# An FNet and GEGLU stack whose scheduler orders by the deadlines of a dry run, with raw operands loaded six items ahead

## The chip, the cores and the metric

The kernel runs on one core of a Trainium2 chip. The metric is the device time of one execution in microseconds; a verdict compares medians of several executions. Times inside an execution come from one profiled execution, whose own time is given beside its span below.

## What is computed

Two kinds of layer alternate, four in all, on `x` of 2048 x 512 in fp32:

```python
def _A_ref(x, dft_seq_re, dft_seq_im, dft_hid_re, dft_hid_im):
    a = jnp.einsum("bsd,ed->bse", x, dft_hid_re)
    b = jnp.einsum("bsd,ed->bse", x, dft_hid_im)
    return jnp.einsum("ts,bse->bte", dft_seq_re, a) - jnp.einsum("ts,bse->bte", dft_seq_im, b)
def _B_ref(x, w_gate, w_up, w_down):
    return (_gelu(x @ w_gate) * (x @ w_up)) @ w_down
x = A_x
x = x + _A_ref(_layernorm(x), ...)    # layer 0
x = x + _B_ref(_layernorm(x), ...)    # layer 1
x = x + _A_ref(_layernorm(x), ...)    # layer 2
x = x + _B_ref(_layernorm(x), ...)    # layer 3
```

The sequence matrices are 2048 x 2048, the hidden ones 512 x 512, gate and up 512 x 1792, down 1792 x 512.

## The kernel before

**Arithmetic.** TensorE works on fp32 operands that are split in two: ScalarE writes the rounded high part (line 140), VectorE subtracts it from the source for the low part (line 141), and `mm3` (lines 174 to 176) adds high x high, high x low and low x high in a PSUM bank. A matmul here takes a 128x128 stationary part and a 128x512 moving part. There are 7034 matmuls in the program, 7002 of them from `mm3`; this text numbers them from 0 in the order in which TensorE runs them.

**Mix layers (0 and 2).** The product with the sequence matrices is done by blocks of seven products in place of eight (Strassen's scheme in Winograd's form). For each of four column blocks b there are the stages A11 and A12, then S2 (with S1 and S3), S4, and between them the products with the hidden matrices (`hid_groups`). All operand blocks of 128x512 fp32 (256 KB) come from memory: `ws` and `wh`. Sums and differences of `ws` blocks are made on VectorE (lines 162 and 165) before they are split. While block b = 3 runs S2 and S4, the normed rows of the next layer come back from memory transposed, as 32 transfers of 64 KB per half (`fetch`, line 612, tensor `t`), and are combined and split too.

**GEGLU layers (1 and 3).** Gate and up are done by seven products per pair of blocks; two halves w of 1024 rows each. The down product is done by seven products for most of the hidden blocks, and by plain products for the rest (`plain_rows`): its first rows wait for `begun` partial sums, which `rows_done` (line 1155, issued by POOL) writes out and `begun_load` (line 1169) reads back in another layout. Eight rows of PSUM results are then added to x (`x_add`, line 165 with a PSUM operand). At the end of layer 1 these rows are normed for layer 2 (lines 494 to 499 and 516, with POOL taking the power at lines 497 and 498) and combined.

**Buffers.** SBUF holds 94 slots of 128x512 (`Slots`, a first-in first-out free list run while the program is traced), and two wide tiles that are lent as eight more (`wide`, `xwide`). PSUM has 8 banks. A tile may be written when the last reader of what was in its slot is done, so a load waits for a matmul or for VectorE.

**The order of the work.** Operands are a list of items in order of use. `split_next` loads up to `RAW` items beyond the one that it splits (`load_next` issues them on SP, line 272), and `take` lets splits run `AHEAD` = 7 items ahead of use. That is the order of the trace. A scheduler then reorders it: it runs the program on a model of the machine and each engine takes the ready instruction that stands first. `machine_as_traced` sets constants of that model: the gap between matmuls and the delay from the issue of a transfer on SP to its start. What comes out is one fixed order for each engine and queue; on the chip every engine runs its own in order and waits on semaphores. So an instruction that waits holds up all behind it on its engine.

Of the kernel before, what the change touches and what calls it, by code (L numbers as in the profile page):

```python
# [24 lines left out]
GELU_C = 0.044715  # L25
AHEAD = 7
MORE = 8
RAW = 4
WARM = 16
LAG = 6  # L30
NEAR = 3, 2, 6
# [7 lines left out]
LEAD = 3  # L39
NK = NS // 2  # L40
PASS_GAP_NS = 13.34
SP_DELAY_NS = 1900


@with_exitstack
def fnet_geglu(ctx: ExitStack, tc: tile.TileContext, x_in, ws, wh, wgu, wdn, wdc, out):
# [216 lines left out]
    def load_next():  # L263
        n = stream["loaded"]
        dtype, addresses, _, _ = items[n]
        raws[n] = []
        for a in addresses:
            t = sb.get(dtype)
            to = t if dtype == F32 else f32(t)
            if len(a.shape) == 3:  # L270
                to = to.rearrange("p (h c) -> p h c", h=2)
            stream["last"] = nc.sync.dma_start(to, a)
            raws[n].append(t)
        stream["loaded"] += 1

    def too_far(n):

        return items[n][2] is whole and n > stream["used"] + items[n][3]

    def split_next():  # L280
        n = stream["split"]
        while stream["loaded"] <= min(n + RAW, len(items) - 1) and not too_far(stream["loaded"]):
            load_next()
# [1047 lines left out]
@contextmanager  # L1331
def machine_as_traced():

    from concourse import hw_specs

    spec = hw_specs.TRN2Spec
    kept = {name: getattr(spec, name) for name in ("PE_FULL_CLOCK_PASS_GAP_NS", "DGE_DMA_DELAY")}
    spec.PE_FULL_CLOCK_PASS_GAP_NS = PASS_GAP_NS
    spec.DGE_DMA_DELAY = {**spec.DGE_DMA_DELAY, mybir.EngineType.SP: SP_DELAY_NS}
    try:  # L1340
        yield
    finally:
        for name, value in kept.items():
            setattr(spec, name, value)
# [43 lines left out]
```

## Time and profile before

| what | value |
|---|---|
| median of three executions | 1645.92 us (1640.87 to 1645.96) |
| profiled execution, its own time | 1644.12 us |
| its span, first to last instruction | 1642.2 us |
| TensorE busy | 1618.0 us, 99% of the span |
| VectorE busy | 1169.2 us, 71% |
| ScalarE busy | 827.5 us, 50% |
| GpSimd (POOL) busy | 229.2 us, 14% |
| moved by DMA | 424.15 MB, mean 258 GB/s |
| mean granted TensorE clock | 0.993 |

TensorE's matmuls overlap: each is shown with its full duration, and the next one starts before it ends. So the number of matmuls in a stretch of time, against the number in a stretch that has no gap, says more than the busy share. "Idle before" of a row is the time that the engine stood still ahead of it, and the arrow names what ended the wait.

### The profile page before, as it was taken

What the parts mean: (1) busy time and instruction counts of PE and PEld (TensorE: products, weight loads), DVE (VectorE), ACT (ScalarE), POOL (GpSimd) and SP (SyncE); (2) the same over time, 40 slices, a digit from 0 to 9 for tenths busy, and PEclk for the clock granted to TensorE, in tenths of its full rate; (3) what the DMA queues carried; (4) which work ended last, traced back from release to release, by engine and by line L of the source; (5) the groups of instructions that cost most, each with busy time, mean ns of one, the idle gap of its engine ahead of it and who ended that gap; (6) DMA issues with size and microseconds to landing.
All of it is one profiled execution on the core that took longest, in us unless ns stands there. A gap on an engine that the chain in (4) does not pass through costs nothing.

```text
span 1642.2 us, 22851 instructions
## 1 busy us (share of the span) xinstructions
PE 1618.0 (99%) x7066; PEld 1329.3 (81%) x7066; DVE 1169.2 (71%) x2009; ACT 827.5 (50%) x1605; POOL 229.2 (14%) x421
## 2 busy tenths in 40 slices
PE   9999999999999999999989999999899999999998
PEld 6888888878788888888878888888688888788887
DVE  8998878778776665657787977787754556944573
ACT  7754454544765535547585533544344545533360
POOL 3111010203544122220230000000001000010002
PEclk9999999999999999999999999999999999999999
DMA  9778787889877799977858777777789676896455
GB/s 363 254 242 275 237 274 230 283 280 359 316 271 263 234 372 368 334 249 237 248 187 299 229 229 241 265 243 259 235 283 312 211 221 184 275 293 204 147 174 154
DMA packets 252106, 424.15 MB, mean 258 GB/s; under 512 B 28816, under 2 KB 91024, under 8 KB 250960
## 3 DMA queue, kind: packets, MB, share of 16 engines
q1 hardware_dynamic: 227232, 336.95, 64.7%
q0 software_dynamic: 24752, 85.74, 14.2%
q8 instruction: 56, 0.92, 0.2%
q14 instruction: 66, 0.54, 0.1%
HBM read 336.86 MB, written 85.72 MB: 257 GB/s over the span
## 4 chain that ended last, share of the span: by engine, by line
PE 79%; DVE 7%; DMA 6%; issue 2%; POOL 1%; ACT 1%; SPq 0%; DVEq 0%; POOLq 0%; ACTq 0%
PE p L174 26%; PE p L175 26%; PE p L176 26%; DVE s L141 4%; DMA s<-ws 1%; DVE s L162 1%; DVE s L165 1%; DMA s<-t 1%; DMA s<-x 1%; DMA out<-s 1%; DMA xwide<-ws 1%; DMA s<-wgu 1%; DMA s<-begun 0%; DMA begun<-wide 0%; DMA begun<-xwide 0%
## 5 line engine op out<-in xcount | busy, mean ns | idle before, releaser
L175 PE MATMUL p<-s,s 128*128 128x512 f32 x2334 | 909.8, 391 | 1.4 <-DVE s L141 1.4
L174 PE MATMUL p<-s,s 128*128 128x512 f32 x2334 | 893.6, 391 | 15.2 <-DVE s L165 7.9
L176 PE MATMUL p<-s,s 128*128 128x512 f32 x2334 | 900.4, 390 | 0.0
L140 ACT ACTIVATE s<-s 128x512 fp32r<-128x512 f32 (+1 forms) x762 | 436.7, 607 | 459.0 <-DVE s L162 143.9
L141 DVE TENSOR_TENSOR s<-s,s 128x512 fp32r<-128x512 f32 (+1 forms) x762 | 482.6, 661 | 103.8 <-ACT s L140 70.3
L174 PEld LDWEIGHTS p<-s,s 128*128 128x128 f32 x2334 | 439.8, 188 | 113.0 <-DVE s L165 10.1
L175 PEld LDWEIGHTS p<-s,s 128*128 128x128 f32 x2334 | 439.8, 188 | 93.9 <-DVE s L141 2.5
L176 PEld LDWEIGHTS p<-s,s 128*128 128x128 f32 x2334 | 439.9, 188 | 91.9 <-issue 0.2
L165 DVE TENSOR_TENSOR s<-s,p 128x512 f32<-128x512 f32 x287 | 192.4, 681 | 174.8 <-PE p L176 79.4
L162 DVE TENSOR_TENSOR s<-s,s 128x512 f32<-128x512 f32 (+1 forms) x310 | 187.2, 618 | 39.7 <-DMA s<-ws 29.9
L169 ACT ACTIVATE s<-p 128x512 f32<-128x512 f32 x214 | 124.8, 590 | 105.6 <-PE p L176 102.7
L903 ACT ACTIVATE s<-s 128x512 f32<-128x512 f32 x103 | 64.8, 629 | 84.1 <-DVE s L165 77.7
L140 ACT ACTIVATE s<-xwide 128x512 fp32r<-128x512 f32 (+1 forms) x96 | 58.6, 617 | 46.8 <-PE p L175 15.6
L141 DVE TENSOR_TENSOR s<-xwide,s 128x512 fp32r<-128x512 f32 (+1 forms) x96 | 64.4, 676 | 14.4 <-ACT s L140 12.2
L497 POOL TENSOR_SCALAR rstd<-rstd 128x1 f32<-128x1 f32 x48 | 17.5, 365 | 392.9 <-ACT s L496 383.8
L165 DVE TENSOR_TENSOR s<-s,s 128x512 f32<-128x512 f32 (+1 forms) x70 | 42.9, 614 | 36.3 <-DMA s<-wgu 19.9
L256 POOL DMA_DIRECT2D wb<-s x84 | 45.8, 547 | 57.2 <-ACT s L140 27.5
L917 DVE TENSOR_TENSOR s<-s,s 128x512 f32<-128x512 f32 x75 | 51.7, 690 | 1.9
L516 ACT ACTIVATE s<-s,shift,rstd 128x512 f32<-128x512 f32 x55 | 44.2, 809 | 7.6 <-DVE shift L489 5.9
L218 POOL DMA_DIRECT2D x<-s x39 | 21.3, 548 | 170.8 <-DVE s L165 169.3
L494 ACT ACTIVATE s<-s 128x512 f32<-128x512 f32 x39 | 24.4, 626 | 36.5 <-DMA s<-x 23.4
L598 DVE STREAM_TRANSPOSE wide<-s 128x512 f32<-128x512 f32 x30 | 21.2, 706 | 25.2 <-ACT s L516 21.2
(98 smaller groups left out, 527.4 us busy)
## 6 DMA issues: line engine op xcount, KB each, us to landing
s<-ws SPq DMA_DIRECT2D x379, 256.0 KB, 4.4
s<-wb SPq DMA_DIRECT2D x294, 256.0 KB, 4.7
s<-wc SPq DMA_DIRECT2D x119, 256.0 KB, 4.3
s<-wh SPq DMA_DIRECT2D x116, 256.0 KB, 4.6
wb<-s POOLq DMA_DIRECT2D x98, 256.0 KB, 4.8
s<-x SPq DMA_DIRECT2D x63, 256.0 KB, 4.8
xwide<-ws SPq DMA_DIRECT2D x58, 256.0 KB, 4.1
wc<-s POOLq DMA_DIRECT2D x49, 256.0 KB, 5.7
```

The lines of the kernel that those rows point to most:

```text
L140: nc.scalar.activation(hi, src, AF.Copy)
L141: nc.vector.tensor_tensor(lo, src, f32(hi), op=ALU.subtract)
L162: nc.vector.tensor_tensor(out, a, b, op=ALU.subtract)
L165: nc.vector.tensor_tensor(out, a, b, op=ALU.add)
L169: nc.scalar.activation(v, src, AF.Copy)
L174: nc.tensor.matmul(ps, ah, bh, start=start, stop=False, skip_group_check=True)
L175: nc.tensor.matmul(ps, ah, bl, start=False, stop=False, skip_group_check=True)
L176: nc.tensor.matmul(ps, al, bh, start=False, stop=stop, skip_group_check=True)
L256: nc.gpsimd.dma_start(a, f32(t))
L516: nc.scalar.activation(z, x, AF.Identity, bias=shift, scale=rstd)
L903: nc.scalar.activation(t, g, AF.Gelu_apprx_tanh)
L917: nc.vector.tensor_tensor(t, t, v, op=ALU.mult)
```

## The change

Four things change. `RAW` goes from 4 to 6. The modelled delay of a transfer on SP goes from 1900 to 3000 ns. The modelled issue queue of VectorE and ScalarE becomes one instruction deep (12 before, by the model's default). And the context is made with `auto_bufs=True`: the scheduler first makes a dry run in the order of the trace, works out from it by when each instruction must have been issued at the latest, and in the final run each engine takes, among its ready instructions, the one with the earliest such deadline; it also assigns the tiles' addresses anew. Nothing else differs, and lines below 42 move down by one, those in and below `machine_as_traced` by more.

```diff
-RAW = 4
+RAW = 6
...
-SP_DELAY_NS = 1900
+SP_DELAY_NS = 3000
+DEPTH = 1
...
-    kept = {name: getattr(spec, name) for name in ("PE_FULL_CLOCK_PASS_GAP_NS", "DGE_DMA_DELAY")}
+    kept = {name: getattr(spec, name) for name in ("PE_FULL_CLOCK_PASS_GAP_NS", "DGE_DMA_DELAY", "ENG_ISSUE_QUEUE_DEPTH")}
     spec.PE_FULL_CLOCK_PASS_GAP_NS = PASS_GAP_NS
     spec.DGE_DMA_DELAY = {**spec.DGE_DMA_DELAY, mybir.EngineType.SP: SP_DELAY_NS}
+    depth = {mybir.EngineType.DVE: DEPTH, mybir.EngineType.Activation: DEPTH}
+    spec.ENG_ISSUE_QUEUE_DEPTH = {**spec.ENG_ISSUE_QUEUE_DEPTH, **depth}
...
-    with machine_as_traced(), tile.TileContext(nc, schedule_with_timeline_sim=True) as tc:
+    with machine_as_traced(), tile.TileContext(nc, schedule_with_timeline_sim=True, auto_bufs=True) as tc:
```

## The prediction

> **What bounds the kernel now.** I read the page first: its first lines, the chain, the costliest groups.
>
> ```profile
> span 1642.2 us, 22851 instructions
> PE 1618.0 (99%) x7066; PEld 1329.3 (81%) x7066; DVE 1169.2 (71%) x2009; ACT 827.5 (50%) x1605; POOL 229.2 (14%) x421
> ...
> PE 79%; DVE 7%; DMA 6%; issue 2%; POOL 1%; ACT 1%; SPq 0%; DVEq 0%; POOLq 0%; ACTq 0%
> ...
> L140 ACT ACTIVATE s<-s 128x512 fp32r<-128x512 f32 (+1 forms) x762 | 436.7, 607 | 459.0 <-DVE s L162 143.9
> L141 DVE TENSOR_TENSOR s<-s,s 128x512 fp32r<-128x512 f32 (+1 forms) x762 | 482.6, 661 | 103.8 <-ACT s L140 70.3
> ...
> s<-ws SPq DMA_DIRECT2D x379, 256.0 KB, 4.4
> ```
>
> TensorE is the bound. The change removes none of its matmuls, so what can be won is the time in which they do not run at full pace. The second view is a table by stretches (length, then busy time and count of each engine, granted clock, DMA share, GB/s).
>
> ```profile
> 40.00:340.00 300.00, 299.88 (x1323) 248.07 (x1322) 256.87 (x445) 153.95 (x292) 38.35 (x65) 1.00 0.79 262
> 340.00:380.00 40.00, 37.18 (x150) 29.79 (x150) 33.82 (x56) 18.25 (x32) 0.00 (x0) 0.91 0.85 255
> 380.00:430.00 50.00, 49.18 (x217) 40.07 (x216) 36.98 (x67) 26.09 (x53) 21.45 (x41) 1.00 0.93 348
> ...
> 510.00:540.00 30.00, 29.24 (x129) 23.75 (x128) 19.09 (x34) 15.82 (x30) 11.84 (x22) 1.00 0.88 284
> ...
> 830.00:870.00 40.00, 35.33 (x147) 28.32 (x146) 36.02 (x76) 36.74 (x85) 12.16 (x16) 0.91 0.51 170
> 870.00:1140.00 270.00, 270.00 (x1193) 223.57 (x1192) 210.24 (x338) 123.00 (x233) 16.53 (x34) 1.00 0.76 249
> 1140.00:1200.00 60.00, 53.40 (x225) 43.34 (x223) 46.92 (x77) 23.28 (x42) 2.17 (x4) 0.94 0.82 257
> 1375.00:1420.00 45.00, 44.13 (x193) 35.68 (x192) 39.70 (x65) 27.13 (x51) 0.00 (x0) 1.00 0.95 279
> ...
> 1600.00:1642.00 42.00, 36.56 (x162) 29.95 (x160) 16.13 (x25) 0.00 (x0) 9.57 (x16) 0.97 0.53 150
> ```
>
> From 870 to 1140 nothing is late: 270 / 1193 = 0.2263 us per matmul. A stretch loses its length less its count times 0.2263: B (340 to 380) 6.1, 380 to 430 0.9, 510 to 540 0.8, C (830 to 870) 6.7, D (1140 to 1200) 9.1, 1375 to 1420 1.3, together 24.9 us. The tail (from 1600) loses 5.3; much of it is the last result's way out. So with everything won the profiled execution's 1644.1 us would be 1619. B, C and D are 21.9 of the 24.9, and in these the clock is below 1: after a long stop the matmuls restart slower.
>
> Third, who ended those stops: the timelines of TensorE, VectorE, ScalarE, POOL and SP.
>
> ```profile
> 360.76 0.39 PE L176 MATMUL p<-s,s 128*128 128x512 f32 x1
> 363.97 0.80 PE L174 MATMUL p<-s,s 128*128 128x512 f32 x1 [2.82 <-DVE xwide L165]
> ...
> 356.75 1.36 DVE L162 TENSOR_TENSOR s<-s,s 128x512 f32<-128x512 f32 x2 [5.31 <-DMA s<-ws]
> 363.24 0.68 DVE L165 TENSOR_TENSOR xwide<-s,p 128x512 f32<-128x512 f32 x1
> 338.69 1.51 SPq L612 DMA_DIRECT2D xwide<-t  x3
> 352.88 4.11 SPq L272 DMA_DIRECT2D s<-ws  x7
> ...
> 1187.56 0.79 PE L174 MATMUL p<-s,s 128*128 128x512 f32 x1 [6.13 <-DVE s L165]
> 1174.77 0.69 DVE L162 TENSOR_TENSOR s<-s,s 128x512 f32<-128x512 f32 x1 [3.42 <-DMA s<-ws]
> 1186.82 1.27 DVE L165 TENSOR_TENSOR s<-s,p 128x512 f32<-128x512 f32 x2
> 1144.22 2.22 SPq L612 DMA_DIRECT2D xwide<-t  x4
> 1181.06 0.38 SPq L272 DMA_DIRECT2D s<-ws  x1
> ```
>
> B and D are the same place of layers 0 and 2. TensorE waits for a PSUM bank that one addition on VectorE (L165 out of p) is to free. VectorE could do it, but stands at an L162 ahead of it, whose `ws` block has not landed though it is used only later. The block is late because SP has issued some twenty small `t` transfers before it. Queue order on two engines, then, makes these stops.
>
> ```profile
> 852.18 0.39 PE L176 MATMUL p<-s,s 128*128 128x512 f32 x1
> 855.80 1.22 PE L174 MATMUL p<-s,s 128*128 128x512 f32 x2 [3.23 <-ACT s L140]
> ...
> 836.25 0.63 ACT L494 ACTIVATE s<-s 128x512 f32<-128x512 f32 x1 [0.23 <-DVE s L165]
> 855.13 0.61 ACT L140 ACTIVATE s<-xwide 128x512 fp32r<-128x512 f32 x1
> 839.59 4.90 POOL L497 TENSOR_SCALAR rstd<-rstd 128x1 f32<-128x1 f32 x1
> 845.17 0.29 ACT L499 ACTIVATE shift<-mean,rstd 128x1 f32<-128x1 f32 x1 [2.52 <-POOL rstd L498]
> ```
>
> C is another case: 18.9 us pass on ScalarE from its first reading of the last rows of layer 1 (836.25) to the split (855.13) that matmul 3656 wants, so TensorE stops at 852.18 + 0.23 = 852.4. Norms and splits wanted hundreds of matmuls later stand ahead of it, and one of them waits for POOL.
>
> **The change part by part.** Both programs hold the same 7034 matmuls and as many instructions on VectorE, ScalarE, POOL and SP; nothing is added but waits. So I compare the built orders. 1518 matmuls move, by 72 places at most. As a measure I count, for each wait of TensorE, the matmuls between the last one that a load had to await before its issue and the one that stands behind that load, through whatever queue: its lead. Least lead, before and after: near matmul 520, 49 and 59; B 58 and 70; near 1755, 69 and 60; near 2230, 50 and 57; C 50 and 99; D 55 and 62; near 6000, 39 and 49. Only one place gets clearly tighter, near 3434: 50 and 34. These leads are long: the median landing of 4.4 us is 19 matmuls.
>
> *Opening, 0 to 40.* The order of x and `ws` changes, the bytes do not. Rows of x come two places sooner. -0.5, bounds -1 and 0.
>
> *B.* SP issues 32 transfers from 338.69 to 356.99, 0.57 us each. The last `ws` load ahead of the addition moves from place 360 to 356 of SP's list, 2.3 us sooner (earlier ones by 12 and 24 places). But the freed bank is now wanted by matmul 1520, not 1526, 6 x 0.2263 = 1.4 us sooner. The stop of 3.2 (360.76 to 363.97) becomes 2.3. The 3.2 is from start to start, less the 0.39 of the pass itself as the row shows it 2.82. The other 2.9 us of B's loss, mostly the slow restart, goes or stays with the clock: 380 to 430 kept 1.00 through 0.9 lost, B lost it after 3.2; 2.3 is nearer to B, so I let it stay: -0.9, bounds -6.1 and +1.4 (only the bank's earlier use).
> The Trainium skill ("TensorE: Matmul & The Clock Gate", What's actually happening) has the clock halved after an idle window of about 3.4 us in a free-running raster; B's 3.2 fits only roughly. By that rule a stop of 2.3 would mostly keep the full clock, and the sum would be some 2.5 us lower, an estimate from that page.
>
> *C.* Between the same two points 26 instructions stand on ScalarE where 36 stood; 18.9 x 26 / 36 = 13.6 us, so the split starts near 849.9 and the matmul's turn, 852.4, is met. Later splits there have 97 to 104 matmuls where 21 to 37 were. -6.7, bounds -6.7 and 0. Late next: POOL (below).
>
> *D.* 52 transfers in 36.8 us (1144.22 to 1181.06) are 0.71 each. The first `ws` loads that VectorE waits for stand 9 to 15 places sooner in SP's list (6 us and more), the last one ahead of the addition only 4 (2.8 us); the bank is wanted 6 matmuls sooner (1.4). By the last alone the stop of 6.1 shrinks by 1.4, by the first ones it goes. Nothing tells which; I take the middle of -1.4 and -9.1, -5. Bounds -9.1 and +1.4.
>
> *380 to 430, 510 to 540, 1375 to 1420.* 3.0 us, leads longer in two of three: half, -1.5, bounds -3 and 0.
>
> *The slot wait near 3434.* RAW = 6 keeps two more items of up to three blocks, up to 6 of 94 slots. So at the end of layer 1 a split's output slot is read until matmul 3427 and the split is wanted by 3434; before, until 3392.
>
> ```profile
> 798.10 6.20 ACT L140 ACTIVATE s<-s 128x512 fp32r<-128x512 f32 x11 [0.41 <-DMA s<-ws]
> 787.16 12.56 SPq L272 DMA_DIRECT2D s<-ws  x12
> ```
>
> Eight splits of just landed `ws` blocks stand ahead of it. Begun at 798.5 as here, at 6.20 / 11 = 0.56 each, they end at 803.0; the split then ends at 803.6, matmul 3434's turn is 802.1: +1.5. Bounds 0 and +10.5 (load issued 8 us after its wait ends, as SP lagged at 1144, landing in 9.0, the longest group of D below).
>
> ```profile
> xwide<-ws SPq DMA_DIRECT2D x1, 256.0 KB, 9.0
> ```
>
>
> *Tail.*
>
> ```profile
> 1610.45 2.74 POOL L1155 DMA_DIRECT2D begun<-xwide  x4 [159.88 <-DVE xwide L165]
> 1631.95 2.24 POOL L1169 DMA_DIRECT2D s<-begun  x4 [8.63 <-DMA out<-s]
> 1637.49 1.36 DVE L165 TENSOR_TENSOR s<-s,p 128x512 f32<-128x512 f32 x2 [1.17 <-DMA s<-begun]
> ```
>
> The last additions wait not for TensorE but for partial sums written out and read back. That begins with the results of matmuls 6908 and 6938; in the new order these are 6916 and 6946, with as many matmuls in all: 8 x 0.2263 = +1.8, bounds 0 and +2.
>
> Sum: -0.5 - 0.9 - 6.7 - 5 - 1.5 + 1.5 + 1.8 = -11.3 on 1644.1: 1632.8. The median shown stands 1.8 above the profiled execution, the lowest 3.3 below it; I add nothing: **1633 us**.
>
> **The rivals.**
> *Transfers bind B and D.* For: DMA shares of 0.82 and 0.85 over them, the same bytes. Against:
>
> ```profile
> 345.00:350.00 5.00, 5.00 (x24) 4.14 (x23) 4.98 (x9) 3.65 (x7) 0.00 (x0) 1.00 0.44 110
> ```
>
> just before B's late loads the engines were half idle. Then B and D keep their losses, each grown by 1.4 as the banks are wanted sooner: 1632.8 + 2.3 + 6.4 = 1641.5.
> *POOL still holds C.*
>
> ```profile
> L497 POOL TENSOR_SCALAR rstd<-rstd 128x1 f32<-128x1 f32 x48 | 17.5, 365 | 392.9 <-ACT s L496 383.8
> ```
>
> The L497 at 839.59 took 4.90 us, the mean of that line is 0.37, and VectorE ran without a gap meanwhile. Four rows pass it. If a second row is held as long, 4.9 less the 2.5 us of margin at C (852.4 - 849.9) makes a stop of 2.4; with a slow restart of as much again, 1638. The Trainium skill ("GPSIMD Engine Reference", Specifications) says that GpSimd's way to SBUF is shared with VectorE and contended by two-input instructions; the long row agrees.
> *Everything goes*, the slot wait too: 1644.1 - 0.5 - 24.9 + 1.8 = 1620.5.
> *Slower: loads late at the slot wait.* With two more items in the queue loads land late; at 3434 the price is 10.5 and 2.5 of slow restart, in place of 1.5. Alone it gives 1644; with B and D unchanged from the same cause, 1653. It decides from a landing some 9 us after SP could issue, twice the median. Against: SP's list near 3434 is nearly that of before.
> *The order hardly matters*: B, C and D stay as they were, near 1645. Against: the leads above.
>
> **How the numbers follow.** About 0.3%, 4.9 us, is what a measurement here can tell from no change: faster ends at 1641.0, slower begins at 1650.9. Forecast 0.52 (1626 to 1640); transfers 0.18, on the border, 0.08 of it faster and 0.10 the same; POOL 0.10, faster; everything 0.08, faster; slower 0.08; order 0.04, the same. Faster 0.78, same 0.14, slower 0.08. The range of 1622 to 1645 leaves out the slower case and half of the best.
>
> **What would show it.** In the profile after: matmuls at 0.2263 and a clock of 1.00 around matmul 3656 (C); an idle time of ScalarE or TensorE's wait for L141 of ScalarE near 3434, of 1 to 2 us; shorter waits of VectorE for `ws` in B and D, and at most 2.3 us of TensorE for L166 in B; a last addition 3 us or more after the last matmul. I am wrong if new stops appear where leads grew, if C's stop is still there, or if B and D are unchanged.

## The result, and the profile after

The kernel after takes 1620.26 us (median; 1618.54 to 1620.53) against 1645.94 us before. The ratio is 0.9843, with a 95% interval of 0.9814 to 0.9872: 1.6% faster. Forecast were 1633 us, so the sign was right and the size half of what came. The profiled execution took 1620.10 us, before it was 1644.12. Lines of the kernel after are higher by one than before (L165 of before is L166 of after). The pages count 7066 matmuls: the 7034 and, ahead of them, 32 of a warm-up, which the numbering leaves out.

First the head of the page of after.

```profile
span 1618.3 us, 22864 instructions
...
PE 1607.9 (99%) x7066; PEld 1325.5 (82%) x7066; DVE 1172.0 (72%) x2009; ACT 827.3 (51%) x1605; POOL 229.0 (14%) x421
...
PE 95%; DMA 2%; DVE 1%; ACT 0%; issue 0%; POOL 0%; SPq 0%; POOLq 0%; DVEq 0%
```

The work of VectorE, ScalarE and POOL is the same to 3 us. What changed is the chain that ends last: 95% TensorE in place of 79%. The table by stretches of after, to hold against the rows that the prediction shows (length, busy time and count of PE, PEld, DVE, ACT, POOL, clock, DMA share, GB/s):

```profile
340.00:380.00 40.00, 40.00 (x178) 33.15 (x177) 34.08 (x57) 19.22 (x34) 2.14 (x4) 1.00 0.96 288
380.00:430.00 50.00, 50.00 (x223) 41.40 (x222) 42.06 (x81) 33.26 (x71) 26.32 (x50) 1.00 1.00 379
510.00:540.00 30.00, 30.00 (x134) 24.86 (x133) 17.67 (x31) 14.59 (x27) 9.65 (x18) 1.00 0.90 298
830.00:870.00 40.00, 40.00 (x178) 33.04 (x177) 33.07 (x63) 33.81 (x72) 7.67 (x11) 1.00 0.66 215
870.00:1140.00 270.00, 270.00 (x1193) 223.58 (x1192) 216.75 (x350) 122.25 (x234) 18.16 (x36) 1.00 0.77 256
1140.00:1200.00 60.00, 60.00 (x267) 49.67 (x266) 45.59 (x74) 24.73 (x43) 0.00 (x0) 1.00 0.88 282
1375.00:1420.00 45.00, 44.95 (x199) 36.83 (x198) 36.43 (x61) 21.46 (x38) 3.91 (x6) 1.00 0.92 300
```

B (340 to 380) holds 178 matmuls where it held 150, C 178 for 147, D (1140 to 1200) 267 for 225, and the clock is 1.00 in all three. The pace itself, 270 / 1193 us, has not moved. The transfers did not get less either: both kernels move 424.15 MB, and in B and D, where more matmuls pass in the same time, the share of the transfers rose from 0.85 to 0.96 and from 0.82 to 0.88. So they did not bind there before.

As after runs ahead of before, clock times compare only roughly. From here on I count by matmul: the loss of a stretch is the time between the starts of its first and last matmul, less their number times 0.2263 us. B, C and D are then matmuls 1440 to 1700, 3600 to 3760 and 4925 to 5200.

| place | loss before, us | loss after, us | change forecast | change measured |
|---|---|---|---|---|
| opening, up to matmul 150 (when that one starts) | 48.36 | 48.93 | -0.5 | +0.6 |
| 150 to 1440 | 0.96 | 0.52 | - | -0.4 |
| B | 6.34 | 0.11 | -0.9 | -6.2 |
| 1700 to 2330 and 5900 to 6200 | 4.51 | 0.75 | -1.5 | -3.8 |
| 3300 to 3600, the slot wait | 0.32 | 1.20 | +1.5 | +0.9 |
| C | 7.20 | 0.11 | -6.7 | -7.1 |
| D | 9.64 | 0.11 | -5 | -9.5 |
| tail, from the start of the last matmul | 6.02 | 7.76 | +1.8 | +1.7 |
| sum | | | -11.3 | -23.9 |

The slot wait near 3434 is there. The rows are TensorE's, ScalarE's and VectorE's timelines of after:

```profile
797.07 0.39 PE L176 MATMUL p<-s,s 128*128 128x512 f32 x1
797.88 0.50 PE L177 MATMUL p<-s,s 128*128 128x512 f32 x1 [0.42 <-DVE s L142]
...
784.66 0.63 ACT L141 ACTIVATE s<-s 128x512 fp32r<-128x512 f32 x1 [0.87 <-PE p L177]
786.70 1.15 ACT L141 ACTIVATE s<-s 128x512 fp32r<-128x512 f32 x2 [1.41 <-PE p L177]
788.06 7.48 ACT L141 ACTIVATE s<-s 128x512 fp32r<-128x512 f32 x14 [0.21 <-PE p L177]
...
788.73 5.51 DVE L142 TENSOR_TENSOR s<-s,s 128x512 fp32r<-128x512 f32 x9
```

ScalarE waits three times for a matmul (`<-PE p L177`): the split's output slot is still read. Then fourteen splits follow without a gap, VectorE subtracts behind them, and the matmul that comes up meanwhile waits 0.42 us for VectorE. It is matmul 3450; at 3434, which the prediction named, 0.2 us are lost. The tail, from the timelines of TensorE, POOL and VectorE of after:

```profile
1610.57 0.39 PE L177 MATMUL p<-s,s 128*128 128x512 f32 x1
...
1607.76 2.23 POOL L1170 DMA_DIRECT2D s<-begun  x4 [8.53 <-DMA out<-s]
...
1610.91 1.30 DVE L166 TENSOR_TENSOR s<-s,p 128x512 f32<-128x512 f32 x2 [9.12 <-DMA s<-begun]
1613.64 1.34 DVE L166 TENSOR_TENSOR s<-s,p 128x512 f32<-128x512 f32 x2 [1.43 <-DMA s<-begun]
```

The last two additions start 3.1 us after the last matmul (1613.64 against 1610.57); before it was 1.3 (1637.49 against 1636.17). They wait for `begun`, as forecast.

VectorE's waits over the whole span fell with B and D (what it waited for: us in total, times, longest). Before:

```profile
DVE s L162 <- DMA s<-ws: 32.2, 18, 6.1
DVE s L165 <- DMA s<-ws: 22.2, 10, 7.1
```

And after:

```profile
DVE s L166 <- DMA s<-ws: 16.5, 11, 2.6
DVE s L163 <- DMA s<-ws: 9.5, 12, 1.6
```

VectorE stood 54.4 us at these two kinds of row for `ws` blocks, and now 26.0; no single wait in these rows is above 2.6 where one was 7.1. With the rows of `xwide` it is 73.8 and 37.9, which is the column W below.

### The profile page after: what moved, and what is told of

Same layout as the page of the kernel before. It is cut to its first block, busy times and chain, and to the rows that moved or that the text cites. A ratio compares the mean times of both kernels' runs of the same rounds, so it can differ in the third digit from the quotient of the medians.

```text
span 1618.3 us, 22864 instructions
## 1 busy us (share of the span) xinstructions
PE 1607.9 (99%) x7066; PEld 1325.5 (82%) x7066; DVE 1172.0 (72%) x2009; ACT 827.3 (51%) x1605; POOL 229.0 (14%) x421
## 2 busy tenths in 40 slices
DMA packets 252106, 424.15 MB, mean 262 GB/s; under 512 B 28816, under 2 KB 91024, under 8 KB 250960
## 4 chain that ended last, share of the span: by engine, by line
PE 95%; DMA 2%; DVE 1%; ACT 0%; issue 0%; POOL 0%; SPq 0%; POOLq 0%; DVEq 0%
PE p L177 32%; PE p L176 31%; PE p L175 31%; PE p L728 1%; DVE s L142 1%; DMA out<-s 1%; DMA s<-begun 0%; ACT s L141 0%; DMA begun<-xwide 0%; DMA s<-t 0%; DMA s<-x 0%; DVE s L166 0%; DVE s L1150 0%; DVE xwide L166 0%; DVE s L163 0%
## 5 line engine op out<-in xcount | busy, mean ns | idle before, releaser
L177 PE MATMUL p<-s,s 128*128 128x512 f32 x2334 | 898.3, 389 | 0.4 <-DVE s L142 0.4
L177 PEld LDWEIGHTS p<-s,s 128*128 128x128 f32 x2334 | 438.2, 188 | 92.7 <-DVE s L142 0.8
L166 DVE TENSOR_TENSOR s<-s,p 128x512 f32<-128x512 f32 x303 | 202.6, 682 | 176.4 <-PE p L177 94.1
L163 DVE TENSOR_TENSOR s<-s,s 128x512 f32<-128x512 f32 (+1 forms) x313 | 188.2, 614 | 16.3 <-DMA s<-ws 9.1
L142 DVE TENSOR_TENSOR s<-xwide,s 128x512 fp32r<-128x512 f32 (+1 forms) x91 | 61.1, 676 | 21.8 <-ACT s L141 12.5
L166 DVE TENSOR_TENSOR s<-s,s 128x512 f32<-128x512 f32 (+1 forms) x61 | 37.4, 615 | 25.5 <-DMA s<-ws 14.3
```

What stands on the lines that cost most here:

```text
L142: nc.vector.tensor_tensor(lo, src, f32(hi), op=ALU.subtract)
L163: nc.vector.tensor_tensor(out, a, b, op=ALU.subtract)
L166: nc.vector.tensor_tensor(out, a, b, op=ALU.add)
L177: nc.tensor.matmul(ps, al, bh, start=False, stop=stop, skip_group_check=True)
```

## The experiments

Each kernel below was compared with the kernel before on the same chip (medians there 1645.67 for e1 to e4, 1646.43 for e5 and e8 to e10, 1642.75 for e6 and e11 to e13, 1645.60 for e14 to e17). "Delay" is the modelled delay of a transfer on SP in ns, "queues" the modelled queue depth of VectorE and ScalarE, "order" whether it is by deadlines. B, C and D are losses in us, W is VectorE's waiting for `ws` blocks in us, all from one profiled execution of each kernel. Where stops are left, executions of one kernel differ by up to 12 us (e16 1629.74 to 1641.47; e9 1640.11 to 1652.47, and its profile is the slowest), so a loss here is one sample, not a mean. e9, e10 and e14 to e17 were built from the kernel after, with the other edits undone; their edits are shown against before (e15's against after), and a queue depth of 12 is the model's default.

| kernel | RAW | delay | queues | order | median, us | ratio to before (95%) | B | C | D | W |
|---|---|---|---|---|---|---|---|---|---|---|
| before | 4 | 1900 | deep | no | 1645.94 | - | 6.3 | 7.2 | 9.6 | 73.8 |
| after | 6 | 3000 | 1 | yes | 1620.26 | 0.9843 (0.9814-0.9872) | 0.1 | 0.1 | 0.1 | 37.9 |
| e1_deadline | 4 | 1900 | deep | yes | 1647.24 | 1.0006 (0.9993-1.0019) | 5.3 | 8.5 | 5.7 | 74.6 |
| e8_raw6_only | 6 | 1900 | deep | no | 1631.59 | 0.9919 (0.9894-0.9945) | 5.8 | 2.8 | 1.5 | 64.3 |
| e9_depth_only | 4 | 1900 | 1 | no | 1647.30 | 1.0002 (0.9981-1.0022) | 6.6 | 0.1 | 10.3 | 77.9 |
| e10_sp_only | 4 | 3000 | deep | no | 1635.92 | 0.9934 (0.9909-0.9959) | 5.2 | 5.5 | 0.1 | 44.8 |
| e2_no_deadline | 6 | 3000 | 1 | no | 1624.56 | 0.9877 (0.9860-0.9893) | 0.1 | 0.1 | 0.1 | 38.4 |
| e3_raw4 | 4 | 3000 | 1 | yes | 1625.22 | 0.9877 (0.9863-0.9892) | 7.1 | 0.1 | 0.9 | 52.9 |
| e4_deep | 6 | 3000 | deep | yes | 1625.29 | 0.9881 (0.9866-0.9896) | 1.1 | 0.4 | 0.1 | 30.4 |
| e5_sp1900 | 6 | 1900 | 1 | yes | 1637.77 | 0.9946 (0.9928-0.9965) | 0.8 | 0.1 | 9.2 | 69.4 |
| e14_raw_sp | 6 | 3000 | deep | no | 1626.21 | 0.9882 (0.9853-0.9911) | 2.9 | 1.0 | 0.1 | 35.3 |
| e16_raw_depth | 6 | 1900 | 1 | no | 1635.33 | 0.9942 (0.9921-0.9962) | 4.0 | 0.4 | 0.5 | 63.2 |
| e17_sp_depth | 4 | 3000 | 1 | no | 1626.25 | 0.9880 (0.9852-0.9909) | 5.3 | 0.1 | 0.1 | 60.8 |
| e15_raw4_sp4000 | 4 | 4000 | 1 | yes | 1619.57 | 0.9840 (0.9806-0.9873) | 1.8 | 0.1 | 0.1 | 44.6 |
| e6_raw5 | 5 | 3000 | 1 | yes | 1621.36 | 0.9864 (0.9846-0.9883) | 0.4 | 0.1 | 0.1 | 46.5 |
| e13_raw5_sp4000 | 5 | 4000 | 1 | yes | 1619.38 | 0.9851 (0.9835-0.9867) | 0.1 | 0.1 | 0.1 | 39.8 |
| e11_t_pool | 4 | 1900 | deep | no | 1644.51 | 1.0007 (0.9992-1.0022) | 4.4 | 8.1 | 7.5 | 73.7 |
| e12_m_pool | 4 | 1900 | deep | no | 1646.83 | 1.0021 (1.0007-1.0036) | 6.6 | 8.0 | 6.4 | 71.1 |

The theory was the prediction's, made sharper: a place loses as its least **lead** is short. (For C of the kernel after the prediction counted a lead of 99, the expectations from e1 on have 91; no conclusion hangs on it.) Its first rival counted the **pace** of the `ws` loads among the t fetches in SP's list.

### One edit taken out, or one alone

**e1_deadline**, the kernel before with one edit:

```diff
-    with machine_as_traced(), tile.TileContext(nc, schedule_with_timeline_sim=True) as tc:
+    with machine_as_traced(), tile.TileContext(nc, schedule_with_timeline_sim=True, auto_bufs=True) as tc:
```

> Only the deadline order is added to the kernel before (RAW 4, 1900 ns and the deep queues stay). Its matmuls stand as before but for 136 rows. Lead theory (a place loses what its least lead is short of, as in the prediction): the leads of B, C and D are 62, 43 and 55 where before has 58, 50 and 55 and after 70, 91 and 62, so C and D stay and B gives a part back: 1640 to 1646. Pace theory (in B and D it counts how evenly the ws loads are spread among the small t fetches in SP's list; the longest row of SP without a ws load in B falls from 19 to 12, as in after, while D goes from 8 to 9): B's 6.2 and the small places behind it go, C and D stay: 1637 to 1640. Deadline theory (the new order is the whole of the change): 1620 to 1625.

Measured: 1647.24, no difference. The order by deadlines alone gains nothing. The pace theory's 1637 to 1640 is missed; D's loss fell to 5.7, but C's rose to 8.5 and 1700 to 2200 to 5.1.

**e2_no_deadline**, the kernel after with that edit undone:

```diff
-    with machine_as_traced(), tile.TileContext(nc, schedule_with_timeline_sim=True, auto_bufs=True) as tc:
+    with machine_as_traced(), tile.TileContext(nc, schedule_with_timeline_sim=True) as tc:
```

> The whole change without the deadline order. Least leads of B, C and D 77, 91 and 68 (before 58, 50, 55; after 70, 91, 62). Lead theory: like after, B, C and D lose nothing, the slot wait near 3434 stays: 1619 to 1623. Pace theory: the longest rows of SP without a ws load are 16 in B and 9 in D (before 19 and 8; after 12 and 5), so B and D keep most of their 6.2 and 9.5 and only C goes: 1633 to 1637. Deadline theory: near before, 1640 to 1646.

Measured: 1624.56. B, C and D are gone without it, and although SP's list in B has a row of 16 transfers without a `ws` load: the pace theory falls. What the deadlines bring to the other three edits, 4.3 us (1624.56 against 1620.26, on two chips; the intervals of the two ratios just overlap), lies between matmuls 1700 and 2200, where e2 loses 3.9 and after 0.2.

**e3_raw4**, the kernel after with

```diff
-RAW = 6
+RAW = 4
```

> The whole change with RAW back at 4. Leads of B, C, D 62, 79, 68, near the slot wait 51 where after has 34. Lead theory: C and D gone, B loses a part, the slot wait of 1.0 gone: 1620 to 1623. Pace theory: rows without ws of 13 in B and 7 in D, near after's: B, C and D gone and the slot wait too: 1618 to 1620. If the six items are what brings the gain: near before, 1640 to 1646.

Measured: 1625.22. B is back whole, 7.1 us, at a lead of 62 and a row of 13: pace falls again, and lead too had allowed less. C and D stay gone.

**e4_deep**, the kernel after with the shallow queues out:

```diff
-    spec.ENG_ISSUE_QUEUE_DEPTH = {**spec.ENG_ISSUE_QUEUE_DEPTH, **depth}
+    pass
```

> The whole change with the modelled issue queues of VectorE and ScalarE as deep as before. Leads of B, C, D 67, 46, 62 where after has 70, 91, 62 and before 58, 50, 55; rows of SP without ws as in after (12 and 5). Lead theory and pace theory alike: B and D stay gone, C comes back with about 7: 1625 to 1629. If the depth is nothing but a detail: 1619 to 1622.

Measured: 1625.29, at the low end of what was expected, but not for that reason: C did not come back (0.4). The 5 us are small ones: 2.8 from 150 to 1440, 1.1 in B, 2.6 behind it, 1.5 near 6000.

**e5_sp1900**, the kernel after with

```diff
-SP_DELAY_NS = 3000
+SP_DELAY_NS = 1900
```

> The whole change but for the modelled delay of a transfer, which stays 1900 ns. Lead theory, now with the bounds that five kernels gave (B lost 5 to 7 at a least lead of 58 to 62 and at most 1 from 67 on; D lost 6 to 10 at 55 and at most 1 from 62 on): leads here are 79 in B, 91 in C, 50 in D, 45 near matmul 520. So B and C stay gone and D comes back with 6 to 10: 1626 to 1631. Stock theory (RAW 6 is what carries B and D): B and D stay gone, 1619 to 1622.

Measured: 1637.77, the largest loss of the four that take one edit out. D is back with 9.2 us, as the lead of 50 said; beyond it 3.5 are lost from 3760 to 4925 (0.4 in after) and 4.3 at the slot wait (1.2), which the lead had not.

**e8_raw6_only**, **e9_depth_only** and **e10_sp_only**, the kernel before with one edit each; in order:

```diff
-RAW = 4
+RAW = 6
```

> The kernel before with RAW 6 and nothing else. Leads 65 in B, 40 in C, 59 in D, 48 near 520, 39 near 6000. Lead theory: B loses about 3, D about 5, C 7 to 9 as before, the small places what they lost: 1634 to 1643. Stock theory: B and D go, C stays: 1628 to 1631.

```diff
+DEPTH = 1
...
+    depth = {mybir.EngineType.DVE: DEPTH, mybir.EngineType.Activation: DEPTH}
+    spec.ENG_ISSUE_QUEUE_DEPTH = {**spec.ENG_ISSUE_QUEUE_DEPTH, **depth}
```

> The kernel before with the modelled issue queues of VectorE and ScalarE one deep and nothing else. Leads 68 in B, 79 in C, 68 in D, 57 near 520, 39 near 6000. Lead theory: B loses at most 1, C and D at most 1, the small places about 3: 1622 to 1627. Stock theory: with RAW 4 B and D stay, at most C goes: 1637 to 1641.

```diff
-SP_DELAY_NS = 1900
+SP_DELAY_NS = 3000
```

> The kernel before with the modelled delay of a transfer at 3000 ns and nothing else. Leads 62 in B, 50 in C, 68 in D, 46 near 520, 42 near 6000. Lead theory: B stays with 5 to 7, C with 7, D goes: 1634 to 1639. Stock theory: B, C and D stay, 1643 to 1648.

Measured: 1631.59, 1647.30 and 1635.92. e9 breaks the lead theory: at leads of 68 in B and in D, both stops are there whole (6.6 and 10.3), and 9.3 more between 1700 and 2200. Its C is gone, 0.1, and yet the sum is zero: what the shallow queues win at C they lose behind B. e10 takes D away, but B and C only in small part. The stock theory (six items carry B and D) falls with e8, where B keeps 5.8. But `RAW` 6 is the edit that alone gains most, 15 us: D falls to 1.5 and C to 2.8.

The profile says what the modelled delay does to D. VectorE's waits for `ws` in e9 and e10, over the whole span, are in the first two and the last two rows:

```profile
DVE s L163 <- DMA s<-ws: 41.1, 23, 6.8
DVE s L166 <- DMA s<-ws: 23.9, 13, 7.5
```

```profile
DVE s L163 <- DMA s<-ws: 21.6, 11, 5.6
DVE s L166 <- DMA s<-ws: 15.4, 8, 6.7
```

And SP's timeline around D, in e9 (where matmul 5066 starts at 1187.0) and in e10 (1176.9), shows the same ten `ws` loads in a row:

```profile
1164.30 2.97 SPq L613 DMA_DIRECT2D s<-t  x4
...
1174.72 5.06 SPq L273 DMA_DIRECT2D s<-ws  x10
1180.12 6.69 SPq L613 DMA_DIRECT2D s<-t  x8
```

```profile
1159.74 4.72 SPq L273 DMA_DIRECT2D s<-ws  x10
1165.11 5.94 SPq L613 DMA_DIRECT2D s<-t  x8
```

They begin 12.3 us ahead of matmul 5066 in e9 and 17.2 us ahead in e10, and in e9 TensorE stops 5.0 us over the pace at matmul 5072. The lists are almost alike, the times are not. What SP waited for on its way to these loads is different too; here are the longest of its rows in e9 (1135 to 1190 us) and in e10 (1095 to 1150):

```profile
SPq L235 <- DVE s L142: 9.8, 1, 9.8
```

```profile
SPq L273 <- PE p L177: 14.9, 12, 6.1
```

In the 80 us ahead of them SP waits 26.8 us for VectorE and 2.7 for matmuls in e9 (1095 to 1176), and 6.9 for VectorE and 19.7 for matmuls in e10 (1085 to 1161). In e10 SP runs as far ahead as TensorE frees slots; in e9 it is held by VectorE, which itself stands at `ws` blocks. So a count of places in SP's list, which is what the prediction used, could not see it.

### Is it one queue? The t and the m loads off SP

SP's waits in the kernel before, 1110 to 1145 us, have one long row ahead of D:

```profile
SPq L234 <- DVE s L141: 7.3, 1, 7.3
```

SP stands 7.3 us at a load of `m_sum` whose slot VectorE has not freed; in e10 the same wait is 1.7. So two more kernels, both the kernel before with one word changed.

**e11_t_pool**:

```diff
-                        nc.sync.dma_start(
+                        nc.gpsimd.dma_start(
                             to.rearrange("p (j t) -> p j t", t=P), cols.rearrange("(j p) t -> p j t", p=32)
                         )
```

> The kernel before, with the 64 small t fetches of each half (line 612) issued by POOL's queue in place of SP's; the other orders stay near before's. In B and D, SP's list then holds ws and wh loads alone. t theory (the prediction's: SP issues some twenty t fetches ahead of the ws loads that VectorE stands at): the stops of B and D go, C stays: 1628 to 1633. m theory (D's ws loads are late because SP stood 7.3 us at an earlier m_sum load, line 234, whose slot was not free): only B goes, D keeps 6 or more: 1636 to 1642. Lead theory: the least lead at D is 44, shorter than before's 55, so D loses 10 or more: 1638 to 1644.

**e12_m_pool**:

```diff
-        nc.sync.dma_start(t, away.pop(key))
+        nc.gpsimd.dma_start(t, away.pop(key))
```

> The kernel before, with the loads of kept sums and differences (m and m_sum, line 234) issued by POOL's queue; SP's list in D is else the same as before, t fetches and all. m theory: SP no longer stands 7.3 us at m_sum, all that follows comes some 7 us sooner, D's 9.6 falls under 3 while B and C stay: 1636 to 1640. t theory and lead theory (lead at D 55 as before): D stays, 1644 to 1648.

Measured: 1644.51 and 1646.83, neither faster. Both theories fall in their strong form. Without t fetches on SP the stops that the prediction read do shrink: the one at matmul 1526 falls from 3.0 us over the pace to 0.8, and the one at 5072 is not there. But two of 1.2 stand at 1529 and 1547, and one of 5.0 at 5013, where TensorE waits for a split on VectorE and not for a bank; so D loses 7.5. Whether 5072 would have stopped without this earlier stop, the run does not tell. With `m` off SP, D falls from 9.6 to 6.4 and not below 3. What took their place in e11, from SP's and VectorE's waits, 1130 to 1186 us:

```profile
SPq L272 <- DVE s L141: 11.2, 7, 8.0
SPq L272 <- DVE s L162: 10.7, 2, 6.9
```

```profile
DVE s L162 <- DMA s<-ws: 10.5, 2, 9.3
```

SP, free of the t fetches, now stands at `ws` loads, 8.0 and 6.9 us, because VectorE has not freed their slots; and VectorE stands 9.3 us at a `ws` block that has not come. Each waits for the other in a fixed order. Taking one member out of this ring passed the wait on.

### Five items, and the whole change with longer leads

**e6_raw5**, the kernel after with

```diff
-RAW = 6
+RAW = 5
```

> The whole change with RAW 5 in place of 6. Leads 61 near 520, 76 in B, 79 at 1755, 67 at 3434, 103 in C, 86 in D, 64 near 6000. The slot wait near 3434 (1.1 in the kernel after) and the last 0.3 near 6000 should go, B, C and D stay gone: 1617.5 to 1619.5. If six items are needed in B as with RAW 4, where 7.1 came back: 1622 to 1627.

**e13_raw5_sp4000**, the kernel after with

```diff
-RAW = 6
+RAW = 5
...
-SP_DELAY_NS = 3000
+SP_DELAY_NS = 4000
```

> The whole change with RAW 5 and the modelled delay at 4000 ns: the longest leads of all built orders (79 near 520, 90 in B, 86 at 1755, 67 at 3434, 105 in C, 86 in D, 67 near 6000). Nothing but the opening and the tail should lose: 1617 to 1619.5. If orders for longer leads cost elsewhere (the opening, the tail): 1620 to 1625.

Measured: 1621.36 and 1619.38. B, C and D are gone in both, near 6000 is 0.12 for 0.49. The slot wait did not go with a lead of 67: e6 loses 2.8 at 3300 to 3600, e13 1.6, after 1.2. So a longer lead of the loads is not what that stop hangs on. With four items it is at most 0.3 in every kernel but e9 (1.9); with five or six it is 0.4 to 4.3. That agrees with the prediction's reason, slots that the additional items keep. e13's interval overlaps after's: no version here is shown to be faster than the kernel after.

### What was still open: lead, or the two edits together

**e14_raw_sp**, the kernel before with

```diff
-RAW = 4
+RAW = 6
...
-SP_DELAY_NS = 1900
+SP_DELAY_NS = 3000
```

> RAW 6 and the modelled delay of 3000 ns, with the deep queues and without the deadline order. Leads 51 near 520, 71 in B, 46 in C, 68 in D. Both-needed theory (B and D go where the six items and the later landings come together): B and D at most 1 each. Depth theory (C goes with the shallow queues alone): C stays with 5 to 8; with the small places 1628 to 1634. If C goes without them as in e4: 1623 to 1627. Lead theory: B and D gone as well.

**e15_raw4_sp4000**, the kernel after with

```diff
-RAW = 6
+RAW = 4
...
-SP_DELAY_NS = 3000
+SP_DELAY_NS = 4000
```

> The whole change with RAW 4 and the modelled delay at 4000 ns. Leads 68 in B, 79 in C, 73 in D. Lead theory: B loses at most 1, 1619 to 1622. Both-needed theory: with four items B stays with 5 to 7 as in e3 (62, 7.1), C and D gone: 1624 to 1627.

**e16_raw_depth**, the kernel before with

```diff
-RAW = 4
+RAW = 6
...
+DEPTH = 1
...
+    depth = {mybir.EngineType.DVE: DEPTH, mybir.EngineType.Activation: DEPTH}
+    spec.ENG_ISSUE_QUEUE_DEPTH = {**spec.ENG_ISSUE_QUEUE_DEPTH, **depth}
```

> RAW 6 and the shallow queues, with the modelled delay of 1900 ns and without the deadline order. Leads 85 in B (more than the kernel after has), 91 in C, 68 in D. Lead theory: B, C and D all gone, 1621 to 1625. Both-needed theory: C goes by the shallow queues, B or D stays with 5 or more: 1628 to 1638.

**e17_sp_depth**, the kernel before with

```diff
-SP_DELAY_NS = 1900
+SP_DELAY_NS = 3000
+DEPTH = 1
...
+    depth = {mybir.EngineType.DVE: DEPTH, mybir.EngineType.Activation: DEPTH}
+    spec.ENG_ISSUE_QUEUE_DEPTH = {**spec.ENG_ISSUE_QUEUE_DEPTH, **depth}
```

> The modelled delay of 3000 ns and the shallow queues, with RAW 4 and without the deadline order. Leads 68 in B, 79 in C, 73 in D. Lead theory: all three gone or at most 1, 1621 to 1625. Both-needed theory: C and D gone, B stays with 5 to 7: 1626 to 1632.

Measured: 1626.21, 1619.57, 1635.33 and 1626.25. e16 settles the lead theory: with 85 in B, more than after's 70, B loses 4.0. But the both-needed theory does not hold strictly either: e14 keeps 2.9 in B, and e15 gets B down to 1.8 with four items, by a later modelled landing still. In e14, C is 1.0 without the shallow queues.

Read by columns, the table says this much:

- **D**: a modelled delay of 3000 or more is enough; with it D loses at most 0.9 in all ten kernels. At 1900 it loses 5.7 to 10.3 in six kernels of eight. It is not the only way: with six items and 1900 it is 1.5 (e8) and 0.5 (e16), but 9.2 in e5.
- **C** is at most 0.4 in all ten kernels with shallow queues, which are enough alone (e9). With deep ones it is 2.8 to 8.5 unless six items and the later landings come together (0.4 and 1.0).
- **B** needs most of the change. It is under 1.2 in the six kernels with five or six items and at least two of the other three edits; with four items it is 4.4 or more but for e15.
- **W**, VectorE's time at `ws` blocks that have not landed, goes with B and D: at 69 or more they lose 10 us or more together, from 52 to 65 it is 4.5 to 8, under 47 at most 5.3, and at most 1.2 in five of the eight.

W goes with B and D over the whole span, but it is not what makes B. From 335 to 365 us VectorE stands at `ws` blocks for 10.6 us in before, 4.8 in after, 7.9 in e2 and 3.5 in e3; yet e2 loses 0.1 in B and e3 7.1. What counts is when the last of these blocks ahead of the addition is there, not how long VectorE has waited in all: VectorE takes it at 362.03 us in before and at 362.65 in e3, while its last wait for one ends at 357.50 in e2 and at 355.90 in after.

So C is shown by one edit (e9), and D by another (e10, and e5 the other way), with the rows that say how. For B the traces show what came sooner (below), but no single edit does it, and which part of the change brings it stays open. So does a count on the built order that tells B ahead of a run; lead, pace and the two-edit rule each missed it in at least one kernel. A kernel in which only the landing of `ws` blocks changes, with every order kept, was not tried.

## Why the prediction was right or wrong

- **What bounds the kernel** was right: the pace stood, and stops with their slow restarts were all that could be won.
- **C** was right in size (-7.1 for -6.7): the whole stop went. That the shorter list of 26 instructions did it is not shown. ScalarE first reads the last rows at 821.64 in after, 23.1 us ahead of matmul 3656 (844.7); before it was 16.2 ahead of its turn (836.25 to 852.4). This earlier start of 6.9 us, which the prediction did not count, is by itself more than the stop of 3.4 us there. POOL did hold ScalarE again, twice, the second time until 2.3 us ahead of matmul 3656, and TensorE did not stop:

```profile
829.77 0.29 ACT L500 ACTIVATE shift<-mean,rstd 128x1 f32<-128x1 f32 x1 [3.47 <-POOL rstd L499]
842.44 0.29 ACT L500 ACTIVATE shift<-mean,rstd 128x1 f32<-128x1 f32 x1 [1.83 <-POOL rstd L499]
```

- **B** is the step that failed first (-6.2 for -0.9). It priced "the last `ws` load ahead of the addition" as 2.3 us sooner: four places of SP's list at 0.57 us each. It was the right load, and its advance is the term that was mis-sized. Here are VectorE's row for that block before, then SP's issue, VectorE's row and the addition after (matmul 1440 starts at 341.20 and 341.33, so the clock times compare):

```profile
362.03 0.69 DVE L162 TENSOR_TENSOR s<-s,s 128x512 f32<-128x512 f32 x1 [0.51 <-DMA s<-ws]
```

```profile
351.76 0.84 SPq L273 DMA_DIRECT2D s<-ws  x2
355.90 0.69 DVE L163 TENSOR_TENSOR s<-s,s 128x512 f32<-128x512 f32 x1 [0.73 <-DMA s<-ws]
357.12 1.28 DVE L166 TENSOR_TENSOR s<-s,p 128x512 f32<-128x512 f32 x2
```

  VectorE has the block 6.1 us sooner (355.90 for 362.03), not 2.3. SP issues it at 351.76 where before it was 356.56, the last of the seven from 352.88. Of these 4.8 us the four places are 1.8; SP stood at the same place 3.0 us sooner than before (351.76 for 354.76), and the block took 4.1 us to land instead of 5.4. Less the 1.4 us by which the bank is wanted earlier, 4.7 us are left, more than the stop of 3.2. So by the step's own sum nothing stays, and nothing restarts slowly. Places times a mean time take it that SP comes to a place when it did before. The question of the clock after a stop of 2.3 us never arose.
- **D** failed by the same term (-9.5 for -5): "only 4 (2.8 us)". Counted from the start of matmul 4925 (1147.18 and 1132.39), that load is issued after 33.9 us before (1181.06) and after 21.9 us in the kernel after:

```profile
1154.30 0.37 SPq L273 DMA_DIRECT2D s<-ws  x1
```

  That is 12.0 us sooner, 8.4 of them because SP stood at the same place sooner. "Nothing tells which; I take the middle" was then a middle between -1.4, which was not true, and -9.1, which was. The cause that the prediction named, t fetches ahead of the `ws` loads, bears on the stops that it read (e11), but taking them off SP moved the loss more than it removed it. The modelled delay alone removes D (e10, 0.1), and `RAW` 6 alone nearly does (e8, 1.5).
- **The small places** failed as "half" (-3.8 for -1.5): all of them went but 0.75.
- **The slot wait** was nearly the right place and the right wait, 0.9 for 1.5. **The tail** was right in kind; that +1.7 meets +1.8 so closely is luck. The five kernels that write `begun` where before does have tails of 5.1 to 6.3 us, the thirteen that do it some eight matmuls later 5.7 to 8.9 (means 5.7 and 7.2). **The opening** had the wrong sign, +0.6 for -0.5; after, the first matmul behind the warm-up starts at 8.16 us, before at 6.79.
- **The rivals.** "Everything goes" gave 1620.5, against 1620.26 measured, and was given a chance of 0.08. All large stops went, as it said; that the sum fits to 0.3 us is partly luck, for the opening and the slot wait cost 2.0 us more than it had, and the stops gave some 2 us more. Its condition had the better reason: leads had grown in B, C and D, and the forecast let B and D keep part of the loss by the count of places alone. Transfers do not bind B and D: with shares of 0.96 and 0.88 both lose 0.1. In the slower rival 1653 adds B and D each grown by 1.4; with both unchanged, as its words have it, it would be 1650.

## What to carry to other kernels

When TensorE's stops come from in-order engines that wait for each other, do not price the advance of a load by its places in the queue's list. Ask what the queue stands at further up (SP at which slot, VectorE at which block): when that changes, the queue comes to the same place sooner, 3.0 us in B and 8.4 in D here. A scheduler's modelled delay of a transfer is such a change. Blocks take 4.4 us from issue to landing, and with 3000 ns in place of 1900 VectorE stands at them for 44.8 us instead of 73.8 (W of e10 and before); that one number was worth 10.5 us alone and 17.5 us in the whole. Edits to a scheduler do not simply add. Alone they gave -15, -11, 0 and 0 us, and that the sum is the -26 of the whole is chance: `RAW` and the delay together gave -19, the delay and the shallow queues -19, `RAW` and the shallow queues -10, and taking one out of the whole cost 4 to 18 us, 32 in all.

## What the runs showed of the hardware

The slow restart does not begin at a fixed length of stop. Over the 18 profiles, counting a stop as the time from start to start less 0.2263 and leaving out those that follow within 40 matmuls of another, all 18 stops of 2.57 us or more were followed by matmuls 0.43 us apart, mostly some ten of them, which cost 1 to 3 us more. Of the eight from 2.07 to 2.55, three were and five were not. Here are a stop of 2.53 in e6 and one of 4.15 in e3, in TensorE's timelines:

```profile
797.25 0.39 PE L176 MATMUL p<-s,s 128*128 128x512 f32 x1
800.00 0.50 PE L177 MATMUL p<-s,s 128*128 128x512 f32 x1 [2.37 <-DVE s L142]
800.34 0.39 PE L175 MATMUL p<-s,s 128*128 128x512 f32 x1
800.57 0.40 PE L176 MATMUL p<-s,s 128*128 128x512 f32 x1
```

```profile
359.62 0.39 PE L177 MATMUL p<-s,s 128*128 128x512 f32 x1
363.99 0.79 PE L175 MATMUL p<-s,s 128*128 128x512 f32 x1 [3.98 <-DVE xwide L166]
364.58 0.63 PE L176 MATMUL p<-s,s 128*128 128x512 f32 x1
365.01 0.63 PE L177 MATMUL p<-s,s 128*128 128x512 f32 x1
...
369.23 0.39 PE L175 MATMUL p<-s,s 128*128 128x512 f32 x1
369.45 0.40 PE L176 MATMUL p<-s,s 128*128 128x512 f32 x1
```

In e6 the next matmuls are 0.34 and 0.23 us apart; in e3 they are 0.59 and then 0.43 apart until 369.23, when the pace comes back within one matmul. The slow stretch need not begin with the restart: behind the stop of 2.07 at matmul 4937 in e1 five matmuls follow 0.34 to 0.23 us apart, and only then some eight 0.43 apart. The Trainium skill ("TensorE: Matmul & The Clock Gate", What's actually happening) lets the clock fall after an idle window of about 3.4 us that runs free of the kernel. That the same 2.45 us slowed one kernel and not another (e5 and e16, both at matmul 3450) agrees with a free-running window; that stops well under 3.4 us are enough does not follow from it.
